# Which PSUM bank a transpose writes: pair 1's and half of the selected rows' go to the banks of the scores

## The chip, the core and the metric

The kernel runs on one core of a Trainium2 chip. Its engines run beside one another and each takes its instructions in order: TensorE (PE; its weight loads are shown as PEld), VectorE (DVE), ScalarE (ACT), GpSimd (POOL), and SyncE (SP), which issues most DMAs. TensorE writes to PSUM only, a memory of eight banks of 128 partitions x 512 floats; VectorE or ScalarE must read a result out before its bank can be written again. The metric is device time in microseconds of one execution; lower is better.

## The reference

Attention with normalized queries and keys, and then a mixture of depths on its result, all in float32:

```python
batch, n_heads, seq, head_dim = (8, 12, 448, 64)
rms = np.sqrt(np.mean(x * x, axis=-1, keepdims=True) + 1e-06)   # q and k: x / rms * g
scores = scale * np.matmul(q_n, k_n.transpose(0, 1, 3, 2))
attn = np.exp(scores - max) ; attn = attn / (sum + 1e-09)
x = np.matmul(attn, v)            # then (B,H,S,D) -> (B, S, H*D) = (8, 448, 768)
# mixture of depths, per batch b, capacity 128, F = 1024:
scores = x[b] @ w_gate
top_idx = np.argpartition(-scores, capacity)[:capacity]
ye = np.maximum(x[b, top_idx] @ w1, 0.0) @ w2
out[b, top_idx] = x[b, top_idx] + sigmoid(scores[top_idx])[:, None] * ye   # the other rows: x
```

## The kernel before

The twelve heads of a batch are taken as three groups of four, so there are 24 groups `n`, each of two pairs of heads `c` (pair 0 and pair 1). A group's keys are cut into seven blocks of 64: a *unit* `u` is one block of one group, 168 units in all.

For a unit, `scores` (L280) issues eight matmuls (L288) into two banks `scs[0]`, `scs[1]`, and ScalarE takes the exponential of each bank (L297) into a tile `p`. `values` (L305) issues eight matmuls (L314) that add `p` times the values into two accumulators over the seven units of a group. `add_probs` (L322) sums the `p` tiles on VectorE (L331) for the denominators.

When a group's seven units are done, `values_out` copies both accumulators to SBUF as `xT` (L341, ScalarE), and `finish` (L638) enters four tasks: `sum_keys` (L352: matmuls L360 into `den_ps`, a ScalarE copy L368), `invert_sums` (L371: two transposes L375 into `denT_ps`, a reciprocal on VectorE, L377), `to_tokens(n, 0)` and `last_tokens(n)`, which begins with `to_tokens(n, 1)`. `to_tokens` (L382) is four transposes of `xT` (L389) into a bank `x_ps`; VectorE multiplies that bank by the reciprocal sums into the token rows `x` (L391). After pair 1, the products with the gate (L415) follow on VectorE, and in every third group the ranking and the selection of 128 rows.

The MoE part of a batch, `mixture` (L506), is a generator that the main loop advances piece by piece. Its first two pieces transpose half of the selected rows `xe` each: three transposes (L523) into a bank, a ScalarE copy (L528) into `xeT`. Then follow the two layers (L542, L561).

Eight banks of PSUM are shared out: four for the scores (`ps_sc`, tag `sc`, used in turn), two for the accumulators (`ps_av`), one `ps_aux`, one `ps_moe`. Two helpers choose a bank. `aux` (L127) serves `den_ps`, `denT_ps`, `x_ps` and `row_ps`:

```python
if PER * now[0] >= units:
    return ps_sc.tile(shape, F32, tag="sc", name=name)
if spare[0]:
    return ps_moe.tile(shape, F32, tag="moe", name=name)
return ps_aux.tile(shape, F32, tag="aux", name=name)
```

The first case is the tail, after the last unit; `spare[0]` is set where the MoE part has no piece to run in this place. `bank` (L512), inside `mixture`, gives `ps_moe`, and a score bank in the tail.

The order of the work is written out by hand: the program keeps, on each engine, the order in which the Python code issues. One turn `q` of the main loop (L727) takes four units: twice (two units of scores, then the values that are due), then `opening(q, 0)`, which runs one task that is due, and then twice (the slots' small work, one piece of the MoE part, and one more task). So all transposes and MoE matmuls of a turn stand behind its scores and values and ahead of the next turn's scores. A tile of a pool with `bufs=4` gets the buffer that was used four tiles ago, and its first writer waits until that buffer's last reader is done.

Of the kernel before, what the change touches and what calls it, by code (L numbers as in the profile page):

```python
# [10 lines left out]
F32 = mybir.dt.float32  # L11
# [57 lines left out]
def fast(  # L69
# [25 lines left out]
    NJ = S // CP  # L95
# [24 lines left out]
    ps_sc = ctx.enter_context(tc.tile_pool(name="ps_sc", bufs=4, space=PSUM))  # L120
# [6 lines left out]
    def aux(shape, name):  # L127
# [6 lines that stand above are left out]
# [24 lines left out]
    ps = ps_moe.tile([128, 512], F32, tag="moe", name="warm_ps")  # L158
# [223 lines left out]
    def to_tokens(n, c):  # L382
        b = n // NG
        if b not in xs:
            xs[b] = x_pool.tile([CP, NJ, DX], F32, name="x")
        t = xTs.pop((n, c))
        ps = aux([128, NJ, 128], "x_ps")
        for j in range(NJ):
            nc.tensor.transpose(out=ps[:CP, j, :], in_=t[:, j, :], identity=ident)  # L389
        col = (n % NG * 2 + c) * 128  # L390
        nc.vector.tensor_tensor(  # L391
            out=xs[b][:, :, col : col + 128].rearrange("p j (h d) -> p j h d", d=D),
            in0=ps[:CP].rearrange("p j (h d) -> p j h d", d=D),
            in1=rdens[n][:, :, :, c, None].to_broadcast([CP, NJ, 2, D]),
            op=OP.mult,
        )
# [109 lines left out]
    def mixture(b):  # L506

        n = CAP
        xe = xes.pop(b)
        xeT = moe_pool.tile([128, NDC, 128], F32, name="xeT")  # L510

        def bank():  # L512

            if PER * now[0] >= units:
                return ps_sc.tile([128, 512], F32, tag="sc", name="sc")
            return ps_moe.tile([128, 512], F32, tag="moe", name="moe_ps")

        half = NDC // 2
        for a in range(2):
            ps = bank()  # L520
            for i in range(half):
                dc = half * a + i
                nc.tensor.transpose(  # L523
                    out=ps[:, 128 * i : 128 * i + n],
                    in_=xe[:n, 128 * dc : 128 * (dc + 1)],
                    identity=ident[:n, :n],
                )
            nc.scalar.copy(  # L528
                out=xeT[:, half * a : half * (a + 1), :n],
                in_=ps[:, : half * 128].rearrange("p (i t) -> p i t", t=128)[:, :, :n],  # L530
            )
            if a == 1:
                row = moe_pool.tile([128, 1], I32, name="row", bufs=2)
                nc.vector.tensor_copy(out=row[:n], in_=xe[:n, DM + 1 : DM + 2])
            yield

        hT = moe_pool.tile([128, NFC, 128], F32, name="hT")
        for f0 in range(0, NFC, 4):
            ps = bank()
            for i in range(4):  # L540
                for dc in range(NDC):
                    nc.tensor.matmul(  # L542
                        out=ps[:, 128 * i : 128 * i + n],
                        lhsT=w1[:, dc, 128 * (f0 + i) : 128 * (f0 + i + 1)],
                        rhs=xeT[:, dc, :n],
                        start=(dc == 0),
                        stop=(dc == NDC - 1),
                    )
                if i == 1:
                    yield  # L550
            nc.scalar.activation(
                out=hT[:, f0 : f0 + 4, :n],
                in_=ps.rearrange("p (i t) -> p i t", t=128)[:, :, :n],
                func=AF.Relu,
            )
            yield
        for a in range(2):
            cols = slice(DM // 2 * a, DM // 2 * (a + 1))
            ps = bank()
            for fc in range(NFC):  # L560
                nc.tensor.matmul(  # L561
                    out=ps[:n, : DM // 2],
                    lhsT=hT[:, fc, :n],
                    rhs=w2[:, fc, cols],
                    start=(fc == 0),
                    stop=(fc == NFC - 1),
                )
                if fc == NFC // 2 - 1:
                    yield
            nc.vector.scalar_tensor_tensor(  # L570
                out=xe[:n, cols],
                in0=ps[:n, : DM // 2],
                scalar=xe[:n, DM : DM + 1],
                in1=xe[:n, cols],
                op0=OP.mult,
                op1=OP.add,
            )
            if a == 1:
                nc.gpsimd.indirect_dma_start(  # L579
                    out=out.flatten_outer_dims(),  # L580
                    out_offset=bass.IndirectOffsetOnAxis(ap=row[:n, :1], axis=0),
                    in_=xe[:n, 0:DM],
                    in_offset=None,
                )
            yield
# [52 lines left out]
    def finish(n, q):  # L638

        if n == n_groups - 1:  # L640
            for fn, args in ((sum_keys, (n,)), (invert_sums, (n,)), (to_tokens, (n, 0))):
                task((q, 1), fn, *args)
            task((q, 1), last_tokens, n)
            return
        task((q, 1), sum_keys, n)
        task((q, 2), invert_sums, n)
        task((q + 1, 0), to_tokens, n, 0)
        task((q + 1, 1), last_tokens, n)
# [6 lines left out]
    def last_tokens(n):  # L655
        to_tokens(n, 1)
        b, g = divmod(n, NG)
        s = soon()
        at(s, gate, n)
        if g < NG - 1:  # L660
            return
        at(s, store_x, b)
        at(s + 1, spread, b)
        q, place = now

        when = (q + 1 + place // 2, 0) if b < B - 1 else (q + 1, 1)
        tasks.insert(0, (when, lambda: ranks_of(b)))
# [45 lines left out]
    def piece(q):  # L713

        nonlocal moe, done
        if next(moe, moe) is not moe:
            return True
        if ready.get(done, q + 1) > q:
            return False
        moe = mixture(done)  # L720
        done += 1
        next(moe)
        return True
# [553 lines left out]
```

## Time and profile before

Three runs took 543.24, 543.69 and 544.44 us, median 543.69. The profiled execution took 543.64 us; its span from the first to the last instruction is 541.9.

| what | from the profile |
|---|---|
| span | 541.9 us |
| scores, L288 on PE | 2688 matmul records, 153.1 us busy |
| values, L314 on PE | 2688 records, 159.2 us |
| x_ps transposes, L389 on PE | 192 records, 29.1 us |
| xe transposes, L523 on PE | 36 records before the tail, 6.1 us |
| reads of x_ps, L391 on DVE | 48, 689 ns each |
| copies of xeT, L528 on ACT | 12 before the tail, 493 ns each |
| exponentials, L297 on ACT | 336, 639 ns each |
| TensorE clock granted, mean | 0.993 of full |

An fp32 matmul of scores, values or of the layers shows as two records, a transpose as one. A PE record's end is modelled and overlaps the next one's start, so starts are compared rather than idle times where PE is concerned. In the timeline, a row is a run of like instructions: start, duration, engine, line, what it writes and reads, how many, and in brackets the idle time before it and what ended that.

### The profile page before, as it was taken

How to read it: one execution, taken by the hardware profiler on the slowest of the kernel's cores; microseconds unless marked ns; L12 is line 12 of the kernel's file. 1: busy time of each engine (PE TensorE's matmuls, PEld its weight loads, DVE VectorE, ACT ScalarE, POOL GpSimd, SP SyncE). 2: the span in 40 equal slices, each digit the busy share in tenths (PEclk: the TensorE clock that was granted, in tenths of full speed). 3: DMA queues.
4: the chain of work that ended last, by engine and by line, in shares of the span. 5: the costliest groups of instructions: out<-in, count | busy, mean ns of one | idle time of the engine just before them, and what ended most of it. 6: DMA issues, size and time to landing. Idle time of an engine off the chain costs nothing. (4 is left out here: it accounts for less than half of the span.)

```text
span 541.9 us, 16470 instructions
## 1 busy us (share of the span) xinstructions
PE 514.9 (95%) x7116; PEld 288.7 (53%) x7116; DVE 339.8 (63%) x644; ACT 278.2 (51%) x506; POOL 242.3 (45%) x193
## 2 busy tenths in 40 slices
PE   6999899999999999999999999999999999999991
PEld 5534344446644375546644466443664456568770
DVE  3767898888475776659557794668746384343000
ACT  3787786784535754446445745547454344311000
POOL 4876988558624176244634456246732103002000
PEclk9999999999999999999999999999999999999997
DMA  8857879999951496508726486605924031004100
GB/s 308 340 164 245 283 245 340 300 304 306 299 181 36 145 256 209 199 31 249 223 101 206 137 250 215 206 2 161 288 86 137 31 104 60 2 20 141 60 4 33
DMA packets 41605, 93.57 MB, mean 173 GB/s; under 512 B 6454, under 2 KB 24374, under 8 KB 41524
## 3 DMA queue, kind: packets, MB, share of 16 engines
q1 hardware_dynamic: 36772, 85.96, 50.1%
q0 software_dynamic: 4608, 6.47, 3.6%
q8 instruction: 58, 0.95, 0.7%
q14 instruction: 23, 0.19, 0.1%
q10 hardware_dynamic: 144, 0.00, 0.0%
HBM read 74.93 MB, written 25.35 MB: 185 GB/s over the span
## 5 line engine op out<-in xcount | busy, mean ns | idle before, releaser
L297 ACT ACTIVATE p<-sc,rinv 128x448 f32<-128x448 f32 x336 | 186.3, 639 | 109.7 <-PE sc L288 88.7
L314 PE MATMUL av<-p,v 64*32 64x448 f32 x2688 | 159.2, 537 | 0.0
L288 PE MATMUL sc<-qT,kT 64*32 64x448 f32 x2688 | 153.1, 540 | 0.3
L212 POOL TENSOR_TENSOR rinv<-ss,neg_half 128x14 f32<-128x14 f32 x48 | 138.6, 2888 | 4.0
L331 DVE TENSOR_TENSOR sum<-sum,p 128x896 f32<-128x896 f32 x113 | 122.5, 1084 | 8.9 <-ACT p L297 1.7
L314 PEld LDWEIGHTS av<-p,v 64*32 64x32 f32 x2688 | 58.7, 107 | 78.1 <-issue 72.0
L209 POOL TENSOR_SCALAR ss<-ss 128x14 f32<-128x14 f32 x48 | 22.8, 475 | 160.4 <-DVE ss L208 134.4
L288 PEld LDWEIGHTS sc<-qT,kT 64*32 64x32 f32 x2688 | 49.4, 106 | 70.0 <-issue 47.4
L542 PE MATMUL moe_ps<-xeT,w 128*128 128x128 f32 x576 | 69.4, 277 | 0.8 <-issue 0.8
L208 DVE TENSOR_REDUCE ss<-sq 128x14 f32<-128x896 f32 x48 | 51.4, 1077 | 29.7 <-ACT sq L202 26.1
L542 PEld LDWEIGHTS moe_ps<-xeT,w 128*128 128x128 f32 x576 | 66.3, 192 | 5.1 <-issue 5.1
L391 DVE TENSOR_TENSOR x<-x_ps,rden 112x512 f32<-112x512 f32 x48 | 32.9, 689 | 55.1 <-PE x_ps L389 50.8
L561 PE MATMUL moe_ps<-w,hT 128*128 128x384 f32 x176 | 61.2, 491 | 0.0
L485 POOL DMA_INDIRECT selected<-x,rank x32 | 36.2, 1131 | 35.0 <-DVE x L477 26.2
L202 ACT ACTIVATE sq<-tok 128x896 f32<-128x896 f32 x48 | 45.9, 962 | 6.8 <-DMA tok<-in_tok_dram 6.7
L579 POOL DMA_INDIRECT out_dram<-xe,row x8 | 10.8, 1354 | 79.8 <-DVE rden L377 47.7
L561 PEld LDWEIGHTS moe_ps<-w,hT 128*128 128x128 f32 x176 | 31.7, 190 | 21.8 <-issue 2.9
L415 DVE SCALAR_TENSOR_TENSOR prod<-x,wg 112x256 f32<-112x256 f32 x96 | 40.9, 426 | 3.0
L226 POOL DMA_DIRECT2D rows<-rinv x44 | 29.1, 662 | 6.6 <-POOL rinv L212 6.5
L389 PEld LDWEIGHTS x_ps<-ident,xT 128*112 128x112 f32 x192 | 21.0, 133 | 18.9 <-issue 12.7
L389 PE MATMUL x_ps<-ident,xT 128*112 128x128 f32 x192 | 29.1, 278 | 1.4 <-DVE x L391 1.4
L570 DVE SCALAR_TENSOR_TENSOR xe<-sc,xe 128x384 f32<-128x384 f32 x5 | 3.1, 618 | 41.0 <-PE sc L561 41.0
(66 smaller groups left out, 339.7 us busy)
## 6 DMA issues: line engine op xcount, KB each, us to landing
tok<-in_tok_dram SPq DMA_DIRECT2D x48, 448.0 KB
qT<-in_qT_dram SPq DMA_DIRECT2D x24, 448.0 KB
kT<-in_kT_dram SPq DMA_DIRECT2D x24, 448.0 KB
v<-in_vp_dram SPq DMA_DIRECT2D x24, 448.0 KB
out_dram<-x SPq DMA_DIRECT2D x8, 1344.0 KB
bc<-rows SPq DMA_DIRECT2D x44, 224.0 KB
xe<-selected SPq DMA_DIRECT2D x8, 385.0 KB
w<-in_moe_w_dram SPq DMA_DIRECT2D x6, 512.0 KB
```

The lines of the kernel that those rows point to most:

```text
L202: nc.scalar.activation(out=sq, in_=t, func=AF.Square, scale=scale)
L208: nc.vector.tensor_reduce(out=ss, in_=sq, axis=AX.X, op=OP.add)
L212: nc.gpsimd.tensor_tensor(out=rinv.rearrange(flat), in0=ss.rearrange(flat), in1=neg_half.to_broadcast([128, 2 * NI]), op=OP.pow,)
L288: nc.tensor.matmul(out=scs[hh][o : o + 32, 0:S], lhsT=get("kT", n)[r, c, D * i + k0 : D * i + k0 + 32], rhs=get("qT", n)[r, c, :], start=True,
L297: nc.scalar.activation(out=p[:, hh], in_=scs[hh][:, 0:S], func=AF.Exp, scale=rinvs[n, 1][:, hh, i : i + 1],)
L314: nc.tensor.matmul(out=avs[n][c][o : o + 32, 0:S], lhsT=get("v", n)[r, hh, i, d0 : d0 + 32], rhs=probs[u][r, hh], start=(i == 0), stop=(i ...
L331: nc.vector.tensor_tensor(out=sums[n], in0=probs[u - 1] if i == 1 else sums[n], in1=probs[u], op=OP.add)
L389: nc.tensor.transpose(out=ps[:CP, j, :], in_=t[:, j, :], identity=ident)
L415: nc.vector.scalar_tensor_tensor(out=prod, in0=xs[b][:, j, cols], scalar=1.0, in1=wg[:, cols], op0=OP.mult, op1=OP.mult, accum_out=gates[b ...
L485: w = nc.gpsimd.indirect_dma_start(out=t[:, :], out_offset=bass.IndirectOffsetOnAxis(ap=rank[:, j : j + 1], axis=0), in_=x[:, j, :], in_of ...
L542: nc.tensor.matmul(out=ps[:, 128 * i : 128 * i + n], lhsT=w1[:, dc, 128 * (f0 + i) : 128 * (f0 + i + 1)], rhs=xeT[:, dc, :n], start=(dc == 0),
L561: nc.tensor.matmul(out=ps[:n, : DM // 2], lhsT=hT[:, fc, :n], rhs=w2[:, fc, cols], start=(fc == 0), stop=(fc == NFC - 1),)
```

## The change

`to_tokens` takes a bank of the scores for pair 1 in place of what `aux` gives; pair 0 goes to `aux` as before. In `mixture`, the second of the two halves of the selected rows takes a bank of the scores in place of `bank()`.

```diff
         t = xTs.pop((n, c))
-        ps = aux([128, NJ, 128], "x_ps")
+        shape = [128, NJ, 128]
+        ps = ps_sc.tile(shape, F32, tag="sc", name="x_ps") if c else aux(shape, "x_ps")
         for j in range(NJ):
             nc.tensor.transpose(out=ps[:CP, j, :], in_=t[:, j, :], identity=ident)
...
         half = NDC // 2
         for a in range(2):
-            ps = bank()
+
+            ps = ps_sc.tile([128, 512], F32, tag="sc", name="xeT_ps") if a else bank()
             for i in range(half):
```

The pools, the order of the instructions on each engine and the DMAs are the same in both. The tiles' sizes are too: an `x_ps` tile is 512 floats to a partition, one bank.

## The prediction

> **What bounds the kernel now.** I read the engine shares first, then the waits, then single places in the timeline.
>
> ```profile
> PE 514.9 (95%) x7116; PEld 288.7 (53%) x7116; DVE 339.8 (63%) x644; ACT 278.2 (51%) x506; POOL 242.3 (45%) x193
> ...
> PEclk9999999999999999999999999999999999999997
> ```
>
> TensorE (PE) is the bound: busy for 95% of the span, at a granted clock that drops only in the tail. VectorE (DVE) has 37% idle, but on average only. A microsecond that PE stands still is a microsecond of time, and a microsecond of waiting elsewhere is nothing. So the waits of PE come next:
>
> ```profile
> PE moe_ps L523 <- ACT xeT L528: 2.1, 3, 1.2
> ...
> PE den_ps L360 <- DVE x L391: 2.1, 5, 0.5
> ...
> PE x_ps L389 <- DVE x L391: 1.4, 3, 0.5
> ```
>
> Columns: total us, times, longest. These are the waits that the change aims at: a bank is needed again before its reader is done. They are 5.6 us of 541.9. In the timeline such a place looks like this (start, duration, engine, line; idle before it in brackets):
>
> ```profile
> 181.64 0.65 PE L389 MATMUL x_ps<-ident,xT 128*112 128x128 f32 x4 [0.46 <-DVE x L391]
> 182.12 0.49 PE L523 MATMUL moe_ps<-ident,xe 128*128 128x128 f32 x3
> 183.07 0.59 PE L360 MATMUL den_ps<-sum,pick_pair 128*32 128x224 f32 x8 [0.45 <-DVE x L391]
> 183.58 1.74 PE L288 MATMUL sc<-qT,kT 64*32 64x448 f32 x32
> ```
>
> The idle numbers understate the loss, since a matmul's record overlaps the next one. I therefore compare starts with the same neighbours elsewhere. Transposes follow one another by 0.11 us (four last 0.60 with 0.27 each); these four started 0.73 after the last xeT transpose: 0.62 lost. den_ps started 0.95 after xeT, where scores follow the same three in 0.42: 0.53 lost.
>
> **What is removed.** By starts, six places lose time that the new banks would free: 118 us (0.53 + 0.26), 181.6 (0.62 + 0.53), 242.7 (0.62), 312.0 (0.80), 372.0 (1.27), 434.3 (0.62 + 0.53): 5.78 us in all. No instruction is added, removed or reordered on any engine; no queue and no DMA is touched. Only banks, and so waits, move. At 44.3 and 103.3 den_ps loses 0.42 each to the read of pair 0, whose bank stays as it is; these stay.
>
> **What takes their place.** Each place is followed to its next wait.
> - 181.6 and 434.3: den_ps then needs only pair 0's read, over 1.49 us earlier, and the next scores' banks are read in time after sliding 1.15. Gain 2 x 1.15 = 2.30.
> - 242.7: PE gains 0.62, but the second score unit's last bank is now pair 1's, whose read ends at 243.56 + 0.68 = 244.24 behind a TENSOR_REDUCE that does not move. The matmul that would start at 244.40 - 0.62 = 243.78 waits until 244.30. Gain 0.10.
> - 372.0: the removed wait hides a second one:
>
> ```profile
> 370.25 0.59 PE L360 MATMUL den_ps<-sum,pick_pair 128*32 128x224 f32 x8
> 372.04 0.55 PE L523 MATMUL moe_ps<-ident,xe 128*128 128x128 f32 x3 [1.20 <-ACT xeT L528]
> ...
> 371.45 0.53 ACT L528 COPY xeT<-moe_ps 128x384 f32<-128x384 f32 x1
> 371.82 0.40 ACT L368 COPY den<-den_ps 128x224 f32<-128x224 f32 x1
> ```
>
> xeT may go at 370.77, but denT right behind it needs ScalarE's den copy, which ends at 372.22; denT starts at 372.27 instead of 372.42. Of 1.27 us 0.15 is left, and 0.13 of that goes to the score bank that xeT now holds, whose copy ends at 373.44. At 312.0 it is the same (0.14 gained, 0.13 lost); at 118 denT's gain of 0.12 is outdone by a wait of 0.24 for the second xeT copy: -0.12. Gain of these three: -0.1.
>
> So 2.3 of 5.8 us remain.
>
> **What is added: scores wait for VectorE.** The score banks rotate over four. Two units of scores fill all four, so one bank taken for pair 1 means that the next unit finds its two, and the unit after it finds one and pair 1's bank. That unit's second matmul now waits until VectorE has read pair 1 (L391). It starts 0.79 us after the first score matmul (two units take 1.50). PE issues in order: behind it stand seven score matmuls, then the values, and behind these the exponentials of ScalarE. So a read that PE didn't wait for at these places now stands before all of that:
>
> ```profile
> 84.98 1.74 PE L288 MATMUL sc<-qT,kT 64*32 64x448 f32 x32
> ...
> 85.80 0.68 DVE L391 TENSOR_TENSOR x<-x_ps,rden 112x512 f32<-112x512 f32 x1
> 86.40 1.07 DVE L208 TENSOR_REDUCE ss<-sq 128x14 f32<-128x896 f32 x1
> 87.40 0.68 DVE L391 TENSOR_TENSOR x<-x_ps,rden 112x512 f32<-112x512 f32 x1
> ```
>
> Pair 1's read ends at 88.08 and is seen 0.06 later (44.26 to 44.32 at den_ps); the matmul stood at 85.77. Price 2.36 us. I took this difference at the 23 places outside the tail. Sixteen are in time, most by 1 to 6 us. Late are 69.6 (read ends 70.90: 1.32), 85.8 (2.36), 304.1 (305.24 against 304.08: 1.22), 284.4 and 365.1 (0.16 each), 134.0 and 387.2 (0.07 each): 5.36. The three large ones share a pattern: no MoE piece runs, so both pairs' transposes stand together and the scores follow 0.5 us behind, while VectorE has a reduce between the two reads. Where a MoE piece of 2.6 us follows, it hides the read at no cost; without that cover, each such place would cost as 304.1 does.
>
> One correction. VectorE is full from 66 to 90 us (5.7 of each 6.0 us), so it slides little when PE loses 1.32 at 69.6, and meets a later PE at 85.8. Full slide leaves 2.36 there, none leaves 1.04; midway between, as its sums do wait for exponentials: 1.7. Added: 1.32 + 1.7 + 1.22 + 0.46 = 4.7.
>
> Sum: 4.7 - 2.3 = **+2.4 us**. The profiled execution took 543.64 (span 541.9 and 1.7 around it), the median is 543.69. Forecast **546.0**.
>
> **Bounds.** The new waits cost at most 5.36, if VectorE slides fully. At least: 69.6's loss can disappear in the 0.98 that PE waits for den at 77.4, and 85.8's in the 2.33 that the values at 89.2 lose; left are 0.34 + 0 + 1.22 + 0.46 = 2.0. The gains lie between 0 and 5.78; I take 2.3, as the next waits are rows. Ends: 2.0 - 2.3 gives 543.3, and 5.4 - 0 gives 549.0; the range leaves a little of both out. The forecast's own range is 544.8 to 547.5.
>
> **Two rules.** The row of the den copy at 371.82 says that a freed bank earns 0.15 of 1.27 us there. The Trainium skill (Perfetto Trace Analysis, Optimization Strategy) reads it otherwise: a gap that repeats on the engine that should be saturated can mean too little PSUM for the next tile. By that rule alone the change would earn all 5.78 us, 537.9. I go by the row.
>
> The granted clock was 1.00 in every stretch up to 480 us, waits of 1.27 us included. The Trainium skill (TensorE: Matmul & The Clock Gate, Why this matters for your kernels) warns that about 3 us of idle TensorE drop it to half speed; no row here shows such a drop behind a wait. An estimate from that page: two such drops of 3.4 us would cost 1.7 us each, 549.4. The longest new wait, 2.36, stays below its bound, and I count nothing.
>
> **Rivals.**
> - *Faster, about 540.9.* VectorE's read of pair 1 is not late, because its reduce slides or the reads of the two pairs close up; then the three large waits fall to a third (1.6) plus 0.5 small ones, and the rows at 118, 312 and 372 give back 2.5 more than I count: 2.1 - 4.8 = -2.7. For it: 5.6 us of waits named in the profile. Against: the reduce has its input early at 86.4, so it stays ahead of pair 1's read, and ScalarE's den copies are in order behind others. It decides at 0.79 us after the first score. Chance 0.09.
> - *No change, about 544.0.* The delays at 69.6 and 85.8 are swallowed by the waits for ScalarE behind them. For it: these waits are there (0.98 and 2.33). Against: ScalarE's work starts from the delayed scores, so it moves too. Chance 0.16.
> - *Slower, about 549.0.* VectorE slides wholly and the freed waits return at denT and at the scores. For it: three of six already do. Against: 181.6 and 434.3 have over 1 us of slack. Chance 0.15.
> - *The banks do not move* (the change does nothing): the pool of the scores has four buffers in use, every second pair takes one of them by name, and at 23 places a later score must then wait for that read; no chance is kept.
>
> The forecast itself has 0.60.
>
> **Numbers.** A measurement of this kernel can tell about 0.2% (1.1 us) from no change; the three runs spread over 1.2. Slower by more than that (above 544.8): 0.60 + 0.15 = 0.75; within it 0.16; faster 0.09. The range is 543.5 to 548.6.
>
> **What would show it.** In the waits: PE or its weight loads at L288 waiting for DVE x L391, three of 1 to 2.4 us at some 70, 86 and 305 us, 4 to 5 us in all. The waits L523 <- ACT xeT and x_ps <- DVE x gone, but denT <- ACT den up by some 2 us. The places at 181 and 434 shorter by 1.15. Wrong if the scores show no wait for VectorE, or if denT starts over 1 us earlier at 312 and 372.

## The result, and the profile after

The kernel before took 543.87 us (median of 4 runs, 543.24 to 544.44), the changed one 543.25 us (4 runs, 542.82 to 544.21). The ratio is 0.9991, with a 95% interval of 0.9974 to 1.0009. That is no change that can be told from none: the interval spans -1.4 to +0.5 us. The forecast was 546.0.

The profiled execution took 543.43 us, its span is 541.7. Its shares and its granted clock:

```profile
PE 516.2 (95%) x7116; PEld 297.0 (55%) x7116; DVE 339.9 (63%) x644; ACT 278.4 (51%) x506; POOL 241.9 (45%) x193
...
PEclk9999999999999999999999999999999999999996
```

The shares are those of before, and the clock drops in the tail only. The waits of TensorE have changed (total us, times, longest; the new lines shift the numbers by one or two, so L392 here is L391 of before, L525 is L523, L530 is L528):

```profile
PE denT_ps L375 <- ACT den L368: 5.2, 7, 1.4
PE sc L288 <- DVE x L392: 2.0, 3, 1.2
PE den_ps L360 <- DVE x L392: 0.7, 2, 0.3
```

The waits of the transposes for `xeT` (2.1) and for `x` (1.4) are gone, and `den_ps` has two of its five left. Three waits of the scores for VectorE's read of pair 1 are new. Those of `denT_ps` stood at 1.8 in three, plus one of 1.4 that the profile of before puts down to VectorE (L415); a later profile of the same kernel, on the third chip below, has them as 3.2 in four. So they are up by 2.0.

First a place that gained. Timeline of after, TensorE, at the place that stood at 181.6 before (start, duration, engine, line):

```profile
182.98 0.65 PE L390 MATMUL x_ps<-ident,xT 128*112 128x128 f32 x4
183.46 0.49 PE L525 MATMUL moe_ps<-ident,xe 128*128 128x128 f32 x3
183.79 0.60 PE L390 MATMUL x_ps<-ident,xT 128*112 128x128 f32 x4
184.23 0.49 PE L525 MATMUL xeT_ps<-ident,xe 128*128 128x128 f32 x3
184.65 0.59 PE L360 MATMUL den_ps<-sum,pick_pair 128*32 128x224 f32 x8
185.16 1.36 PE L288 MATMUL sc<-qT,kT 64*32 64x448 f32 x24
```

From the first transpose to the scores it takes 2.18 us; before it was 183.58 - 180.20 = 3.38. The gain is 1.20, and it is the same at 434 us.

Next the place at 372, where the forecast saw a second wait behind the one removed. Of the same timeline:

```profile
371.58 0.59 PE L360 MATMUL den_ps<-sum,pick_pair 128*32 128x224 f32 x8
372.10 0.55 PE L525 MATMUL xeT_ps<-ident,xe 128*128 128x128 f32 x3
373.58 0.43 PE L375 MATMUL denT_ps<-ident,den 128*112 128x128 f32 x2 [0.93 <-ACT den L368]
```

The second `xeT` starts 0.52 after `den_ps` and no longer 1.79 after it. But `denT_ps` comes 2.00 after `den_ps`, where it came 2.17: 0.17 gained of 1.27, and 0.10 of it is lost again behind.

Last the largest of the new waits, and what follows it:

```profile
87.17 1.69 PE L288 MATMUL sc<-qT,kT 64*32 64x448 f32 x18
90.11 0.60 PE L288 MATMUL sc<-qT,kT 64*32 64x448 f32 x7 [1.24 <-DVE x L392]
...
93.93 2.92 PE L314 MATMUL av<-p,v 64*32 64x448 f32 x48
96.78 0.59 PE L360 MATMUL den_ps<-sum,pick_pair 128*32 128x224 f32 x8
```

The second matmul of the second unit should start at 87.17 + 0.79 = 87.96 and starts at 90.11: 2.15 lost, where 2.36 was the price at full slide (VectorE delayed as much as TensorE). VectorE's read is the reason:

```profile
88.38 1.08 DVE L208 TENSOR_REDUCE ss<-sq 128x14 f32<-128x896 f32 x1
89.37 0.68 DVE L392 TENSOR_TENSOR x<-x_ps,rden 112x512 f32<-112x512 f32 x1
```

It ends at 90.05 and is seen 0.06 later. Now the same values in the timeline of before:

```profile
89.20 4.79 PE L314 MATMUL av<-p,v 64*32 64x448 f32 x48
93.92 0.58 PE L360 MATMUL den_ps<-sum,pick_pair 128*32 128x224 f32 x8
```

48 value records took 4.72 us to the start of `den_ps` before, and 2.85 after. (Of the time won, the scores ahead of them take a part back: the last 31 records took 2.62 us from 91.31 in after, the last 32 took 1.94 before.) The piece of work from the first score to `den_ps` took 93.92 - 84.98 = 8.94 us before and 96.78 - 87.17 = 9.61 after. A wait of 2.15 us has added 0.67. This piece of work takes 6.63 us where nothing slows it (second chip, below); it is the slow stretch of the following sections. So here is where the forecast's loss went, and the experiments are about this place above all.

### The profile page after: what moved, and what is told of

Read it like the earlier page. It is cut to its first block, busy times and chain, and to the rows that moved or that the text cites. A ratio compares the mean times of both kernels' runs of the same rounds, so it can differ in the third digit from the quotient of the medians.

```text
span 541.7 us, 16469 instructions
## 1 busy us (share of the span) xinstructions
PE 516.2 (95%) x7116; PEld 297.0 (55%) x7116; DVE 339.9 (63%) x644; ACT 278.4 (51%) x506; POOL 241.9 (45%) x193
## 5 line engine op out<-in xcount | busy, mean ns | idle before, releaser
L288 PE MATMUL sc<-qT,kT 64*32 64x448 f32 x2688 | 160.3, 541 | 2.2 <-DVE x L392 2.0
L314 PE MATMUL av<-p,v 64*32 64x448 f32 x2688 | 162.2, 537 | 0.1
L314 PEld LDWEIGHTS av<-p,v 64*32 64x32 f32 x2688 | 63.3, 107 | 71.2 <-issue 58.7
L288 PEld LDWEIGHTS sc<-qT,kT 64*32 64x32 f32 x2688 | 53.5, 106 | 72.5 <-issue 44.2
L392 DVE TENSOR_TENSOR x<-x_ps,rden 112x512 f32<-112x512 f32 x48 | 32.9, 689 | 54.0 <-PE x_ps L390 49.6
L341 ACT COPY xT<-av 128x448 f32<-128x448 f32 x48 | 23.4, 549 | 11.2 <-PE av L314 7.8
```

The lines of the kernel that those rows point to most:

```text
L288: nc.tensor.matmul(out=scs[hh][o : o + 32, 0:S], lhsT=get("kT", n)[r, c, D * i + k0 : D * i + k0 + 32], rhs=get("qT", n)[r, c, :], start=True,
L314: nc.tensor.matmul(out=avs[n][c][o : o + 32, 0:S], lhsT=get("v", n)[r, hh, i, d0 : d0 + 32], rhs=probs[u][r, hh], start=(i == 0), stop=(i ...
```

## The experiments

They ran on three chips, and the kernel before takes 543.4, 534.2 and 543.9 us there. Each ratio is against runs of the kernel before on the same chip. The letters of the theories are explained in the expectations themselves. The edits stand against the kernel before, and none leaves out or changes any of the computation.

### First chip: is the slow stretch chance, and do the parts add up?

The kernel before once more, to see which differences between the two profiles are chance.

> The kernel before once more, for a second profile. Theory A (the wait for VectorE near 86 us is given back because the values at 89 us run slowly in the kernel before for a fixed reason of that place): the 24 values at 89 us again take about 4.7 us where 2.26 is usual, and the 1.0 us hole among the L542 matmuls near 207 us is there too. Rival B (such slow stretches come and go by chance from run to run, and the changed kernel's profile was lucky): one or both are missing or have moved. Both: 543.2 to 544.5 us.

It took 543.98 us. From the first score at 86.07 to `den_ps` at 95.00 are 8.93 us again, so the slow stretch belongs to the kernel. A hole of 1.0 us in the row of L542 at 208 us, which the profile of before has and that of after hasn't, is absent here (and there again, 1.2 us, in a later profile on the third chip): it comes and goes without an edit and is no gain of the change. Against this profile the end of after is 0.32 earlier.

Then the change in two halves. One keeps `ps_moe` for pair 1 wherever no MoE piece runs, which takes away the three large new waits:

```diff
+        score_bank = c == 1 and not spare[0]
+        ps = ps_sc.tile(shape, F32, tag="sc", name="x_ps") if score_bank else aux(shape, "x_ps")
...
+            ps = ps_sc.tile([128, 512], F32, tag="sc", name="xeT_ps") if a else bank()
```

> The change without its banks in the turns that have no MoE piece (pair 1 takes the MoE bank there as before), so the three waits of scores for VectorE at 70, 88 and 305 us (1.33 + 2.15 + 1.23) go. Theory A: the freed waits earn 2.8 and the slow values at 89 us stay as before: 541.0 us, ratio 0.995. Rival B: against the changed kernel's 543.25 all 4.7 is gained: 538.6. Rival C (the waits were not what held the change back): no faster than the changed kernel, 543.2.

Measured: 540.77 against 543.37, ratio 0.9953 (0.9939 to 0.9968), that is -2.6 us. By the shifts of TensorE's starts against the second profile of before (minus is earlier): 118 us -0.54 and +0.44, 134 +0.33, 182 to 184 -1.20, 242 -0.61, +0.57 and -0.31, 285 +0.19, 366 +0.15, 434 to 436 -1.20. No wait of the scores for VectorE's `x` is left in its list:

```profile
PE denT_ps L375 <- ACT den L368: 5.2, 7, 1.4
...
PE den_ps L360 <- DVE x L393: 0.7, 2, 0.3
```

The other half uses a score bank only where `ps_moe` was free, and leaves `xeT` as it was:

```diff
+        score_bank = c == 1 and spare[0]
+        ps = ps_sc.tile(shape, F32, tag="sc", name="x_ps") if score_bank else aux(shape, "x_ps")
```

> Only the turns without a MoE piece take a score bank for pair 1; everything else as before. Theory A: the waits at 70 and 305 us cost 1.33 + 1.23, the one at 86 some 0.2 net: 546.5 us, ratio 1.005. Rival B: all three cost in full, 4.7: 548.6, ratio 1.0086. Rival C: the waits cost nothing: 543.9.

Measured: 546.18 against 543.37, ratio 1.0055 (1.0039 to 1.0072), +2.8 us. Its waits have the three that the other half lacks:

```profile
PE sc L288 <- DVE x L393: 2.0, 3, 1.2
```

The trace has +1.33 at 70, +2.15 and +0.66 at 87 to 89 and then -2.0 up to 95, +1.14 at 304 and -0.50 at 328. The halves sum to +0.2; the whole is -0.6 with an interval of -1.4 to +0.5. So the change is a gain of 2.6 and a loss of 2.8 that cancel, and not an edit without effect.

The wait at 86 alone:

```diff
+        score_bank = c == 1 and n == 3
+        ps = ps_sc.tile(shape, F32, tag="sc", name="x_ps") if score_bank else aux(shape, "x_ps")
```

> One tile alone: pair 1 of group 3 takes a score bank, which makes the one wait near 86 us. Theory A: PE waits 2.1 to 2.4 us there and gets it back by 95 us, since the values at 89 us then run at their usual pace: 543.9 to 544.3 us, shift of PE after 100 us below 0.5. Rival B: the shift stays at 2.1 to 2.4: 546.1.

Measured: 544.62 against 543.37, ratio 1.0019 (1.0006 to 1.0033), +1.25 us. By starts +2.37 and +0.56, then -1.37, -0.31 and -0.31: 0.95 stays. Some 1.4 of the 2.37 are given back, less than theory A said and far more than B.

### Second chip: the same edits where the stretch isn't slow

Pair 1 alone, and the selected rows alone:

```diff
+        score_bank = c == 1
+        ps = ps_sc.tile(shape, F32, tag="sc", name="x_ps") if score_bank else aux(shape, "x_ps")
```

> The change's first edit alone: every pair 1 takes a score bank, the second half of the selected rows stays in the MoE bank. Theory A: the three waits cost 2.6 to 2.8 net as in the run with these alone, and the places at 182 and 435 us earn 0.8 each instead of 1.2, since the second xeT half has to wait for the first one's copy: 543.4 + 2.7 + 0.5 - 1.9 = 544.7 us, ratio 1.0025. Rival E (the two edits do not need one another): the places earn 1.2 each as with both, ratio 1.000.

```diff
-            ps = bank()
+            ps = ps_sc.tile([128, 512], F32, tag="sc", name="xeT_ps") if a else bank()
```

> The change's second edit alone: the second half of the selected rows takes a score bank, pair 1 stays. Theory A: the 0.26, 0.80 and 1.27 us that PE waits for the xeT copy at 119, 312 and 372 us come back as waits of denT for ScalarE's den copy and of a score bank for the second xeT copy: 543.3 to 543.5 us, ratio 1.000. Rival E: they are gained: 541.1, ratio 0.9957.

Measured: pair 1 alone 535.73 against 534.21, ratio 1.0027 (1.0014 to 1.0040); the rows alone 534.86, ratio 1.0007 (0.9995 to 1.0019). The bank of `xeT` earns nothing by itself: at 118, 312 and 372 the den copy stands behind, and at 181 and 434 the bank of pair 1 is still missing. Pair 1 alone earns 0.78 and 0.70 there by starts against the rows alone, near the 0.8 expected. That its ratio meets theory A's 1.0025 is in part luck: the wait at 86 is given back at another place than A had it.

The traces show more than was asked. In the four profiles of this chip the slowness at 89 doesn't occur. From the first score to `den_ps`, the kernel before on the third chip, in the table by windows (columns: window, length, busy us and instructions of PE, PEld, DVE, ACT and POOL, granted clock, DMA share, GB/s):

```profile
85.92:94.91 8.99, 8.99 (x130) 3.71 (x129) 7.99 (x15) 5.62 (x11) 7.61 (x7) 1.00 1.04 343
```

The same view of the rows alone:

```profile
86.14:92.77 6.63, 6.63 (x129) 2.69 (x128) 6.40 (x14) 5.53 (x11) 5.25 (x7) 1.00 1.04 320
```

The work is the same to a record (128 scores and values and the first one or two records of `den_ps`), the granted clock is 1.00 in both, and TensorE never stands idle. It is 2.36 us slower in one. The same holds at 139 us, where the timeline of before has 32 values in 4.50 us:

```profile
137.75 4.50 PE L314 MATMUL av<-p,v 64*32 64x448 f32 x32
```

The timeline of the rows alone has them in 1.71, with the selection writes beside them as in before (TensorE, then GpSimd):

```profile
139.56 1.71 PE L314 MATMUL av<-p,v 64*32 64x448 f32 x32
...
138.08 0.97 POOL L485 DMA_INDIRECT selected<-x,rank  x1 [0.30 <-issue]
139.36 1.08 POOL L485 DMA_INDIRECT selected<-x,rank  x1 [0.30 <-issue]
```

With the stretch at full pace, another limit decides a little later. ScalarE's timeline with the rows alone:

```profile
105.95 0.95 ACT L202 ACTIVATE sq<-tok 128x896 f32<-128x896 f32 x1 [4.08 <-DMA tok<-in_tok_dram]
```

And with pair 1 alone:

```profile
104.83 0.95 ACT L202 ACTIVATE sq<-tok 128x896 f32<-128x896 f32 x1
```

Without the new waits ScalarE stands 4.08 us at a load of tokens, and TensorE's scores wait behind it for an exponential (1.4 us idle in its list). With them, `den_ps` is 2.99 later at 95 us (95.76 against 92.77) and still at 105 (105.16 against 102.17), but `denT_ps` behind this place comes at 112.23 against 111.71: 0.52. So 2.5 us of the loss go at this load. It doesn't move with TensorE: it is issued at about 99.5 us in both. But it has landed by 104.8 with the waits and lands near 105.9 without, so some 1.1 of the 2.5 may be the load's own earlier arrival.

Is the slow stretch tied to GpSimd's selection writes (L485)? Four of them stand at 85.5 to 90.8 us in the profile of before, the first and the last of them here:

```profile
85.51 1.31 POOL L485 DMA_INDIRECT selected<-x,rank  x1 [0.30 <-issue]
...
89.65 1.10 POOL L485 DMA_INDIRECT selected<-x,rank  x1 [0.30 <-issue]
```

Four more begin up to 7 us ahead of each of the later places where scores or values run slowly (138, 261, 328, 391 and 451 us), so the slowness comes beside the writes or just behind them. At 202 and 495 us such writes stand beside matmuls of the MoE layers instead. The selection of batch 0 was therefore put later, first alone and then with the wait at 86:

```diff
-        at(s + 2, select, b)
-        at(s + 8 if s >= 0 else s + 3, load_selected, b)
+        at(s + 5 if b == 0 else s + 2, select, b)
+        at(s + 12 if b == 0 else s + 8 if s >= 0 else s + 3, load_selected, b)
```

> The kernel before with GpSimd's four selection writes of batch 0 three slots later (about 6 us) and their load four slots later; the banks are as before. Theory D (the values at 89 us run slowly because these four writes are being issued at that time): the values at 89 us take about 2.3 us instead of 4.7, and if there is a slow stretch it stands where the writes now are, near 93 to 99 us. Rival F (the stretch belongs to that place in the program or to the weight loads): it stays at 89 us with 2.0 lost. The time tells little: 541.4 to 543.4 us by D, 543.4 by F.

> Pair 1 of group 3 alone in a score bank (the one wait near 86 us) together with the later selection writes. Theory D: there is no slow stretch behind the wait that could give it back, so the shift of PE against the kernel with the later writes is the whole 2.1 to 2.4 us at 95 us. Rival F: 0.9 us, as with the writes in their old place.

Measured: 533.38, ratio 0.9983 (0.9970 to 0.9997), and with the wait 534.49, ratio 1.0009 (0.9995 to 1.0022). As no profile of this chip shows the slowness, the first can't say what the writes do to it. The pair does say what the wait costs at full pace: 8.77 us from the first score to `den_ps` against 6.63, so 2.14 are paid on the spot. By `denT_ps` at 110, also counted from the first score, 1.57 are left (25.24 against 23.67): the token load held ScalarE for 2.18 us in the first of the two and not at all in the second. The times differ by 1.1.

### Third chip: the writes, the two other waits, and a better version

The kernel before once more took 545.19 us; it has the slow stretch (8.99 us, above).

> The kernel before on the chip of these runs, for a profile to set theirs against. If this is the first chip (543.4 us): slow values at 89, 139, 391 and 451 us again. If it is the second one (534.2): these stretches run at their usual pace, and PE instead waits some 2.9 us between 104 and 116 us, ScalarE standing for a token load first, as in the run with the second edit alone.

The waits at 70 and 304 without that at 86 (`n in (2, 14)` in place of `n == 3`):

> Pair 1 of groups 2 and 14 alone in a score bank: the waits near 70 and 305 us without the one near 86. Theory A (a wait of PE counts in full unless a limit that doesn't move with PE stands right behind it; behind these two there is at most the 0.47 at 327 us): 1.33 + 1.22 less up to 0.5, ratio 1.004 to 1.005, more than the wait near 86 alone although that is as long as both together. Rival H (a third or more of any wait is given back): 1.003 or less.

Measured: 546.44 against 543.88, ratio 1.0041 (1.0026 to 1.0056), +2.6 us. By starts +1.35 and +1.23, and -0.44 at 329. Two waits that sum to 2.6 us cost all but 0.44 of it, while 2.37 us in one wait at 86 cost 0.95 by starts (1.25 by the times). The interval alone would still allow the 1.003 of rival H; the starts don't.

Score banks only at the places that gain (`score_bank = c == 1 and n in (8, 11, 20)` for pair 1, `a == 1 and b in (1, 2, 5)` for the rows):

> The score banks only where a freed wait is not followed by another: pair 1 of groups 8, 11 and 20 and the second half of the rows of batches 1, 2 and 5. Theory A (these three places, 1.2 + 0.4 + 1.2, are the change's whole gain): ratio 0.995. Rival G (the gain of the version without the three waits is spread over all places): 0.998 or above.

Measured: 541.45 against 543.88, ratio 0.9940 (0.9922 to 0.9958), -2.4 us, by starts -1.20 at 183, -0.34 at 243 to 248 and -1.20 at 436. Three places are the whole gain.

And the first half of the change (`score_bank = c == 1 and not spare[0]`, and the rows) with the later selection writes of batch 0:

> The version without the three waits, together with the later selection writes of batch 0. If the two are independent: 0.9953 x 0.9983 = 0.9936. If the later writes only moved a slow stretch that this version loses or keeps anyway: 0.9953.

Measured: 540.30, ratio 0.9929 (0.9911 to 0.9947), the lowest median on this chip; next to the three places the intervals overlap. The 0.9936 expected of two independent gains is met, but by luck: the 0.9983 in it comes from the chip without the slowness. TensorE, then GpSimd, in its timeline:

```profile
88.95 2.52 PE L314 MATMUL av<-p,v 64*32 64x448 f32 x47
...
94.72 2.34 PE L314 MATMUL av<-p,v 64*32 64x448 f32 x32
...
90.53 1.60 POOL L487 DMA_INDIRECT selected<-x,rank  x1 [0.20 <-issue]
92.43 1.76 POOL L487 DMA_INDIRECT selected<-x,rank  x1 [0.30 <-issue]
94.50 0.94 POOL L487 DMA_INDIRECT selected<-x,rank  x1 [0.30 <-issue]
95.75 1.52 POOL L487 DMA_INDIRECT selected<-x,rank  x1 [0.30 <-issue]
```

The writes now begin 4.1 us later than in the kernel before on this chip (86.45). The stretch at 89 is at full pace (6.63 us from the first score to `den_ps`), and the values beside the third and fourth write take 2.34 for 32, where 1.71 is usual. So in this one run the slowness moved with the writes, at a smaller size: against the first half alone (on the first chip) 2.3 us are gained by `den_ps`, and 1.1 of them lost again in the 5 us from 95 on.

All kernels side by side ("shown" are the two profiles that the result compares), from the first score behind pair 1's transposes to `den_ps`, by starts:

| kernel | chip | wait at 86 | us |
|---|---|---|---|
| before (three profiles) | shown, 1st, 3rd | none | 8.94, 8.93, 8.99 |
| first half; three places; 70 and 304 only | 1st; 3rd; 3rd | none | 8.93; 8.99; 8.89 |
| after; second half; 86 alone | shown; 1st; 1st | 2.14 to 2.37 | 9.61; 9.74; 9.88 |
| first half, later writes | 3rd | none | 6.63 |
| rows alone; later writes | 2nd | none | 6.63; 6.63 |
| pair 1 alone; 86 and later writes | 2nd | 2.14; 2.37 | 8.54; 8.77 |

At full pace the wait adds 1.91 and 2.14 us, in the slow stretch 0.67 to 0.95.

## Why the prediction was wrong

**What was right.** The change moves only waits, and they lie where they were placed. The three large new waits came at 69.7, 87.2 and 303.7 us with 1.32, 2.15 and 1.21 us, for 1.32, 2.36 and 1.22 at full slide. The gains at 181 and 434 are 1.20 each for 1.15. At 118, 312 and 372 next to nothing is left, as `denT_ps` takes over: its waits are up by 2.0, for "some 2". At 242 the 0.61 gained is taken back by 0.57 at the next scores, as foreseen, though 0.31 comes back behind it. In sum the first half of the change, small new waits included, was worth -2.3 + 0.46 = -1.8 by the working and measured -2.6, with an interval of -3.3 to -1.7.

**The step that failed** is the price of the new waits, "Added: 1.32 + 1.7 + 1.22 + 0.46 = 4.7". Its three large terms, 4.24, measured 2.8 (2.1 to 3.9). The term for 85.8 is the worst: 1.7 was counted and 0.67 to 0.95 is paid where the stretch is slow. The reason given for 1.7, that VectorE would slide only half, was wrong as well: it slid nearly whole, and the wait was 2.15. What the sum lacked is that the work behind the wait was itself running slowly and runs faster when it comes later. The next term, 1.22 at 304, lost 0.44 to 0.50 at 328 us, where 29 scores took 2.0 us before (1.5 is usual) just behind selection writes; that the reason is the same there is likely, not tested. Of the 3.0 us between the forecast +2.4 and the measured -0.6, these waits make up 1.4 and the larger gain of the first half 0.8; the remaining 0.8 is within the spread of the halves.

**The bound that held it.** The forecast's low end did let "85.8's in the 2.33 that the values at 89.2 lose" vanish, but read those 2.33 as a wait that would move with TensorE, and so it was kept out of the likeliest case. That this end, 543.3, meets the measured 543.25 is luck: it also let 0.98 of the wait at 69.6 vanish, which stayed, and it counted too little gain. The rival "no change" had the place right and the limit wrong: the delay was not swallowed by waits for ScalarE. TensorE is busy throughout in the slow stretch (8.99 of 8.99 us). At 69.6 nothing was swallowed: 1.33 was still there at 85 us.

**The two rules.** The Trainium skill (Perfetto Trace Analysis, Optimization Strategy) says that a repeated gap can mean too little PSUM; taken alone, that would have given all 5.78 us. With more banks in use 2.6 were gained, as at three of six places another wait ended at nearly the same time. The warning of the Trainium skill on idle TensorE (TensorE: Matmul & The Clock Gate, Why this matters for your kernels) met no case: no new wait reached its 3 us, the longest being 2.37, and the granted clock is 1.00 in after from 85 to 95 us, the wait of 2.15 included.

**What stays open.** Why scores and values slow down near the selection writes on two chips and not on the third isn't settled, nor is it shown that the writes are the cause. The writes of one batch were moved on the third chip once, and together with the first half of the change; on the second chip the same writes at the same place cost nothing. That VectorE read pair 1 ahead of its reduce, which would take the new waits away at their root, was not tried.

## What to carry to other kernels

A bank borrowed from a rotating pool makes a later user of that pool wait for the borrower's reader, and on an engine that works in order everything behind it waits too; so lend only where the reader is done in time, place by place: here pair 1 of three groups in 24, with the rows of three batches, is the whole gain. To price a new wait, follow it to the next limit and ask whether that limit moves with the delayed engine: a transfer, or a stretch that was running slowly, gives time back, and a chain that starts from the delayed work does not. And run the halves of a change that measures as nothing: this one is -2.6 and +2.8.

## What the runs showed of the hardware

- The same kernel takes 543.4, 543.9 and 534.2 us on three chips, at the same granted clock (0.99 in the mean on each). In the one place compared closely the difference is a slower run of the same matmuls with TensorE busy throughout: 8.99 against 6.63 us.
- The records of scores and values otherwise start in groups of eight (four matmuls), all within some 0.1 us, one group every 0.375 us. In the slow stretches of before, on the first and third chips, values start singly or by twos and threes, many of them 0.3 to 0.4 us apart, with next to no wait in the profile and the granted clock at 1.00. In the one run on the third chip in which four indirect writes of GpSimd came 4.1 us later, the slowness came later too; that run also had the first half of the change, which alone, on the first chip, left the stretch at 8.93 us.
